# Wider mode products, one product for x, and shorter products on zeros in a windowed-attention and spectral-mixing kernel

## The chip, the cores and the metric

The kernel runs on one core of one Trainium2 chip. The metric is the device time of one execution in microseconds; the median of several executions counts. The engines are named as in the profile: PE is TensorE (PEld its weight loads), DVE is VectorE, ACT is ScalarE, POOL is GpSimd, and SP is SyncE, which only issues DMAs here.

## The reference

The kernel computes windowed causal attention and then mixes its output over the sequence in the frequency domain. Cut to what matters:

```python
# q, k, v: (8 batches, 8 heads, 576 positions, 64)
scores = where(0 <= i - j < 64, q @ k.T / 8, -1e9)
x = (softmax(scores) @ v), heads side by side    # (8, 576, 512)
X = rfft(x, axis=1)[:, :64]                       # 64 modes, Xr and Xi
Yr[m] = Xr[m] @ w_r[m] - Xi[m] @ w_i[m]           # w_r, w_i: (64, 512, 512)
Yi[m] = Xr[m] @ w_i[m] + Xi[m] @ w_r[m]
y = irfft(Y, n=576)
u = x + y
out = u + max(u @ w_ch, 0)                        # w_ch: (512, 512)
```

All inputs and the output are float32 in memory. The weights of the modes are 2 x 64 x 512 x 512 numbers, by far the most of what is read.

## The kernel before

The program is one stream per engine, in an order written out by hand; each engine runs its instructions in that order and waits on semaphores between engines.

**Products on zeros.** Right at the start (L428 to L432) a stretch of Yall is set to zero, and PE multiplies it with itself WARM = 8 times, 512 columns each, into a PSUM tile that nobody reads. Meanwhile SP fetches k and q of the first group as float32 (load_by_sp, L419), DVE computes the table of sines and then casts them (L426), and POOL issues the other loads.

**Attention (until about 196 us).** Sixteen groups (8 batches by two halves of the heads) pass through. transpose_raw (L292) turns k, q and v on PE in products of 64 columns (L298), and ACT copies them out (L302). The scores (L345), the subtraction of the maximum (L357), the turned weights (L365) and the product with v (L385) follow, and do_dft (L402) multiplies each finished half batch with the tables of cosines and sines, into XQ[0] and XQ[1], for the lower and upper 256 channels. All loads go through POOL's queue (load, L281, and load_weights, L150), cast to bfloat16 on the way. In POOL's order a load of k, q or v waits until PE has turned what lay in its buffer, and a load of weights until its buffer is spent.

**Modes.** A group is four modes. For every mode the weights are multiplied from the lower and upper channels (hb) and for the real and imaginary part (ri). Three forms of product exist. Each puts several products side by side on PE by tile_position, which gives each of them its own columns of the array:

- mode_half (L217), for the lower channels of groups 0 to 9 and the upper ones of groups 0 and 1: four modes side by side, 32 columns of weights each.
- mode_wide (L231), for the upper channels of groups 2 to 9 (WIDE = 2, EARLY = 10). The 256 rows of two modes lie interleaved, so that each load writes whole partitions; one tile of moving data holds both modes. The stationary side comes from XE, which holds one copy of X for the even and one for the odd mode (index h), with zeros in the rows of the other mode. For each of the NW = 4 slices j and each of the four modes g there is one product with 32 stationary columns: 16 products for each call, and 16 calls.
- mode_pair (L244), for the groups from 10 on.

The 32 columns are four slots of 8 batches. Slot by slot XE holds -Xi, Xr and Xi for each j, three slots each, and a product takes four slots in a row, from Xr on for ri = 0 and from -Xi on for ri = 1. The first two of the four are the answer, the last two are never read. wide_modes (L721) fills XE once, at about 202 to 207 us: products with a spreading matrix (L730), then a memset (L735), copies by ACT (L740) and negated copies by DVE (L741).

Between the mode products PE prepares the end: it turns tiles of x (L678), multiplies them with w_ch (L685), and DVE keeps the results as XW (L942). load_weights keeps POOL's queue filled; a load goes out when its ring buffer is free.

**Tail (from about 394 us).** After the last weights, 36 tiles of 128 positions are finished in pairs. For a pair PE brings XW into PSUM (L976), adds the inverse transform (L986, L993, L1033, L1063), and DVE, ACT and POOL add and store. rows_u (L1025) brings x itself into PSUM by a product with the identity, for the 12 tiles that are not in add_x: two products of 256 columns, one for each half of the channels (L1029), ahead of the inverse transform of the same tile (L1033). SP sends the finished tiles out (L1003).

Of the kernel before, what the change touches and what calls it, by code (L numbers as in the profile page):

```python
# [13 lines left out]
ALU = mybir.AluOpType  # L14
# [2 lines left out]

NRA = 3
NRB = 5
WARM = 8  # L20
NEG = -1.0e30
MAGIC = 12582912.0
PSAFE = 3.14159
# [3 lines left out]
def kernel(  # L27
# [10 lines left out]
    nc = tc.nc  # L38
    B, H, S, D = q.shape
# [9 lines left out]
    HALF = DM // 2  # L49
    NJ = 2  # L50
    NW = DM // 128
# [16 lines left out]
    ident_bf = consts.tile([128, 128], BF16, name="ident_bf")  # L68
# [19 lines left out]
    XQ[1] = post.tile([128, 3 * NJ + 2, B, NM], BF16, name="XQ1")  # L88
    XE = XQ[1].rearrange("p s b m -> p (s b m)")
    Yall = post.tile([2 * NM, B, DM], BF16, name="Yall")  # L90
# [14 lines left out]
    WIDE = 2  # L105
    NE = 2 * (EARLY - WIDE)
    SHARES = 25, 11, 80, 12
    assert sum(SHARES) == 128
    XE = XE[:, 0:2 * (3 * NW + 2) * B * NE].rearrange("p (h s b m) -> p h s b m", h=2, b=B, m=NE)
    ONES = 3, 0  # L110
    wlist = []
    for at, (grp, hb) in enumerate(steps):
        for ri in range(2):
            p = 4 * grp
# [26 lines left out]
    wtiles, spent = {}, set()  # L141
# [72 lines left out]
    def spend(at, ri):  # L214
        spent.update(i for i, w in enumerate(wlist) if w[0] == at and w[3] == ri)
# [15 lines left out]
    def mode_wide(psm, at, ri):  # L231
        grp, hb = steps[at]
        for j in range(NW):
            for g in range(4):
                nc.tensor.matmul(out=psm[32 * g:32 * g + 32, :],  # L235
                                 lhsT=XE[:, g % 2].rearrange("k s b m -> k (s b) m")[:, (3 * j + 1 - ri) * B:(3 * j + 5 - ri) * B,
                                                                                    2 * (grp - WIDE) + g // 2],
                                 rhs=wtiles[4 * grp + g - g % 2, hb, ri][:, j], start=(ri == 0 and j == 0),
                                 stop=(ri == 1 and j == NW - 1), tile_position=(0, 32 * g))
        for i in range(2):  # L240
            wtiles.pop((4 * grp + 2 * i, hb, ri))
        spend(at, ri)
# [19 lines left out]
    with tc.manual_schedule():  # L262
# [165 lines left out]
        idle = Yall[:, 0, :]  # L428
        nc.vector.memset(idle, 0.0)
        warm = ps_m.tile([128, DM], FP32, name="warm", tag="misc")  # L430
        for _ in range(WARM):
            nc.tensor.matmul(out=warm, lhsT=idle[:, 0:128], rhs=idle, start=True, stop=True)  # L432

        casts = list(load_by_sp(0, "k", Vflat[1])) + list(load_by_sp(0, "q", Vflat[2]))
        nc.gpsimd.iota(Kf, pattern=[[1, 64]], base=0, channel_multiplier=0,
# [11 lines left out]
        for nm in ("k", "q", "v"):  # L447
# [17 lines left out]
                         op0=ALU.max, op1=ALU.min)  # L465
# [82 lines left out]
        for it in range(-3, NU + 3):  # L548
# [23 lines left out]
            g = starts.get(it + 2)  # L572
# [3 lines left out]
            g = starts.get(it + 1)  # L576
# [34 lines left out]
        def bank(h, shape=(128, DM), dtype=FP32, name=None):  # L611
            return banks[h].tile(list(shape), dtype, name=name or "ps" + h, tag="bank")
# [50 lines left out]
        def group_y(b):  # L663
            return 32 * ((b // 2 + 2) % 4)
# [4 lines left out]
        def yrows(b):  # L669
            return Yall[:, b, :]  # L670
# [50 lines left out]
        def wide_modes():  # L721
            nc.vector.memset(sprE, 0.0)
            for r in range(2):
                for h in range(2):
                    nc.vector.tensor_copy(out=sprE[:, r, h, h::2], in_=ident_bf[:, r::2])
            pts = [[bank("zt"[r == 0]) for j in range(NJ)] for r in range(2)]
            for r in range(2):
                for j in range(NJ):
                    for h in range(2):
                        nc.tensor.matmul(  # L730
                            out=pts[r][j][:, 2 * B * NE * h:2 * B * NE * (h + 1)], lhsT=sprE[:, r, h],
                            rhs=XQ[1][:, 3 * j + 1:3 * j + 3, :, 4 * WIDE:4 * EARLY].rearrange(
                                "p t b (m h) -> p (t b) m h", h=2)[:, :, :, h],
                            start=(h == 0), stop=True, skip_group_check=True)
            nc.vector.memset(XE[:, :, 3 * NW:], 0.0)  # L735
            for r in range(2):
                for j in range(NJ):
                    i = 3 * (NJ * r + j)
                    px = pts[r][j].rearrange("p (h t b m) -> p h t b m", h=2, t=2, b=B)
                    nc.scalar.copy(out=XE[:, :, i + 1:i + 3], in_=px)  # L740
                    nc.vector.tensor_scalar(out=XE[:, :, i], in0=px[:, :, 1], scalar1=-1.0, scalar2=None, op0=ALU.mult)  # L741
            lo = 4 * (LAST - EARLY)
            nc.vector.tensor_copy(out=XL, in_=XA[:, :, :, lo:lo + 8])

# [180 lines left out]
        tiles = []  # L925
# [33 lines left out]
        ps, pu = {}, {}  # L959
# [65 lines left out]
        def rows_u(of):  # L1025
            for i in of:
                if i not in add_x:
                    for h in range(2):
                        nc.tensor.matmul(out=pu[i][:, HALF * h:HALF * h + HALF], lhsT=ident_bf, rhs=tiles[i][0][:, h],  # L1029
                                         start=(h == 0), stop=True, skip_group_check=True)  # L1030
                if len(tiles[i][1]) == 1:
                    (at, b), = tiles[i][1]
                    nc.tensor.matmul(out=pu[i], lhsT=trigI[:, at:at + 128], rhs=yrows(b), start=(i in add_x), stop=True,  # L1033
                                     skip_group_check=True)
            for i in of:
                if len(tiles[i][1]) == 2:
                    for h, (at, b) in enumerate(tiles[i][1]):
                        nc.tensor.matmul(out=pu[i][64 * h:64 * h + 64], lhsT=trigI[:, at + 64 * h:at + 64 * h + 64], rhs=yrows(b),
                                         start=(i in add_x), stop=True, skip_group_check=True, tile_position=(0, 64 * h))
            for i in of:  # L1040
                b = tiles[i][1][0][1]
                if len(tiles[i][1]) == 2 and b < NLB:
                    r = slice(group_y(b), group_y(b) + 32)
                    nc.tensor.matmul(out=pu[i], lhsT=trigX[r], rhs=YL[r], start=False, stop=True, skip_group_check=True,
                                     tile_position=(group_y(b), 0))
# [32 lines left out]
        def full_u(n):  # L1078
            banks_u(n)
            ut = uts[n] = new_ut()  # L1080
            joint = len(tiles[seq[n][0]][1]) == 2
            for of in [seq[n]] if joint else [(i,) for i in seq[n]]:
                rows_u(of)
                for i in of[0:1]:
                    take_rows(i, ut[:, seq[n].index(i)])
            tail_xw(n)
# [22 lines left out]
        def last(n):  # L1109
            banks_u(n)  # L1110
            ut = new_ut()
            ut = [ut[:, j] for j in range(2)]
            for j, i in enumerate(seq[n]):
                rows_u((i,))
                take_rows(i, ut[j])
            for j, i in enumerate(seq[n]):
                tail_xw(n, (j,))
                rows_z(i)
                for lo in range(0, DM, HALF * (2 - j)):
                    hi = lo + HALF * (2 - j)  # L1120
                    nc.vector.scalar_tensor_tensor(out=ut[j][:, lo:hi], in0=ps[i][:, lo:hi], scalar=0.0,
                                                   in1=ut[j][:, lo:hi], op0=ALU.max, op1=ALU.add)
                    done[i] = ut[j]
                    put_out(nc.scalar if lo else nc.sync, i, lo, hi)
# [8 lines left out]
        for i, (grp, hb) in enumerate(steps[EARLY:]):  # L1133
            if i == WIDE - 1:
                whole_modes()
            if i == WIDE:
                wide_modes()
# [13 lines left out]
            psm = bank("m")  # L1151
# [51 lines left out]
        for h, ps_ in enumerate(zl):  # L1203
            for c in range(NDCH):
                nc.tensor.matmul(out=ps_[:, 0:HALF], lhsT=trz[:, c].rearrange("p g k -> p (g k)"),
                                 rhs=wch[:, c, HALF * h:HALF * h + HALF], start=(c == 0), stop=(c == NDCH - 1))
# [8 lines left out]
        for g in (2, 3):  # L1215
            nc.sync.dma_start(out=Zall.bitcast(FP32)[rows, 2 * g:2 * g + 2],
                              in_=ZL.bitcast(FP32)[32 * g:32 * g + 32])
# [43 lines left out]
```

## Time and profile before

| | |
|---|---|
| median of 3 runs | 430.47 us (430.37 to 432.55) |
| profiled execution, its time | 430.37 us |
| its span, first to last instruction | 428.6 us |
| mean granted TensorE clock | 0.909 |
| PE busy, PE weight loads busy | 341.0 us (80%), 224.9 us (52%) |
| DVE, ACT, POOL busy | 247.1, 184.6, 113.2 us |
| DMA moved | 93.30 MB, 81.80 of them on POOL's queue |

A row of the timeline gives start, duration, engine, line, operation, the tile written and the tiles read, partitions and columns of the weights (128*32 is 128 rows and 32 columns), the shape written, and the count; in brackets stands how long the engine had been idle and for what. Where several instructions are merged into one row, the duration is that from the first start to the last end. A product's own duration includes the time that it takes to run through the array, so that products follow each other in less than one duration. A row of the chain of waits gives start, length and what the end was waiting for at that time. The windows view gives each engine's busy time in a stretch, the granted TensorE clock, and the DMA share, which is over 1 where packets overlap.

### The profile page before, as it was taken

Reading aid. Unit: us, or ns where it says so; the run is one execution under the profiler, and the core shown is the slowest. Engines: PE = TensorE matmul, PEld = TensorE weight load, DVE = VectorE, ACT = ScalarE, POOL = GpSimd, SP = SyncE. Lnnn points to the kernel's source line nnn. Section 1 sums busy time; section 2 is a strip of 40 time slices with the busy share of each in tenths; the row PEclk is TensorE's granted clock in tenths of the full one; section 3 lists DMA queues with packets and bytes.
Section 4 is the critical chain, followed back from the end, with each engine's and each line's share of the span. In section 5 each row is a group of like instructions: output and inputs, shape, how many; then the busy total and the mean of one; then the engine's idle time right before and its main releaser. Section 6 shows DMA issues by size and latency. Waiting matters only on the chain.

```text
span 428.6 us, 11742 instructions
## 1 busy us (share of the span) xinstructions
PE 341.0 (80%) x5098; PEld 224.9 (52%) x5142; DVE 247.1 (58%) x527; ACT 184.6 (43%) x334; POOL 113.2 (26%) x174
## 2 busy tenths in 40 slices
PE   6889989898999998987628577669675668878994
PEld 3656767676767676663204233346454445445552
DVE  8688777877677675784503212033322333886995
ACT  5655757575676566532401101025222214233663
POOL 8313223222122132112222222121111111120994
PEclk9999999999999999985657767689999986999998
DMA  8999999999999999999999999999999999996698
GB/s 206 211 211 212 211 212 210 212 211 212 211 211 212 213 213 210 213 213 214 213 255 220 213 213 214 207 211 214 214 215 214 214 214 214 213 210 119 241 364 299
DMA packets 37188, 93.30 MB, mean 218 GB/s; under 512 B 2992, under 2 KB 3248, under 8 KB 37136
## 3 DMA queue, kind: packets, MB, share of 16 engines
q0 software_dynamic: 31424, 81.80, 97.9%
q1 hardware_dynamic: 5568, 10.62, 6.8%
q8 instruction: 40, 0.66, 0.6%
q10 hardware_dynamic: 144, 0.13, 0.1%
q14 instruction: 12, 0.10, 0.1%
HBM read 163.58 MB, written 9.44 MB: 404 GB/s over the span
## 4 chain that ended last, share of the span: by engine, by line
DMA 43%; PE 39%; DVE 8%; issue 6%; ACT 3%; POOL 0%; DVEq 0%; SPq 0%; POOLq 0%; ACTq 0%
DMA wr<-in_moe_w_r_dram 23%; DMA wi<-in_moe_w_i_dram 16%; PE tr L298 6%; PE s L345 5%; DMA rawk<-in_k_dram 4%; PE s L357 4%; PE pt L365 4%; PE vb L310 3%; PE o L385 3%; PE s L337 2%; PE psm L223 2%; PE psz L685 2%; PE psm L254 2%; DVE xw L888 1%; PE px L408 1%
## 5 line engine op out<-in xcount | busy, mean ns | idle before, releaser
L685 PE MATMUL psz<-wch,tr 128*128 128x512 f32 x176 | 58.6, 462 | 10.8 <-DMA wch<-in_moe_w_ch_dram 10.0
L349 DVE TENSOR_REDUCE mx<-s 128x4 fp32r<-128x512 f32 x72 | 49.6, 688 | 25.5 <-PE s L345 25.2
L942 DVE CAST xw<-psz 128x512 fp32r<-128x512 f32 x36 | 24.9, 692 | 67.7 <-PE psz L685 67.7
L653 ACT CAST tr<-ptx 128x512 fp32r<-128x512 bf16 x36 | 21.2, 590 | 78.4 <-PE ptx L678 78.4
L359 ACT ACTIVATE p<-s 128x512 bf16<-128x512 f32 x72 | 39.7, 603 | 13.0 <-PE s L357 13.0
L685 PEld LDWEIGHTS psz<-wch,tr 128*128 128x128 f32 x176 | 34.4, 216 | 17.4 <-issue 10.2
L345 PE MATMUL s<-kT,qT 64*64 64x128 bf16 (+1 forms) x576 | 29.2, 221 | 6.7 <-issue 6.7
L302 ACT COPY kT<-tr 128x576 bf16<-128x576 bf16 x32 | 23.2, 724 | 21.4 <-PE tr L298 21.4
L368 DVE COPY pts<-pt 128x1024 bf16<-128x1024 bf16 (+1 forms) x40 | 25.2, 630 | 5.8 <-PE pt L365 4.3
L302 ACT COPY qT<-tr 128x576 bf16<-128x576 bf16 x32 | 23.3, 727 | 11.5 <-PE tr L298 11.5
L235 PEld LDWEIGHTS <-XQ 128*32 128x32 bf16 x256 | 11.4, 147 | 31.9 <-issue 25.5
L345 PEld LDWEIGHTS <-qT 64*64 64x64 bf16 x576 | 18.0, 107 | 17.7 <-issue 17.2
L357 PE MATMUL s<-mx,ident_r 128*128 128x512 f32 x72 | 26.2, 437 | 0.0
L302 ACT COPY vT<-tr 128x576 bf16<-128x576 bf16 x32 | 23.3, 728 | 4.7 <-PE tr L298 4.5
L285 POOL DMA_DIRECT2D rawk<-in_k_dram x15 | 8.1, 538 | 64.3 <-PE tr L298 56.3
L365 PE MATMUL pt<-ident_bf,p 128*128 128x128 bf16 x288 | 23.3, 220 | 1.8 <-issue 1.6
L747 DVE TENSOR_TENSOR stg<-psm,Yfour 128x512 bf16<-128x512 f32 x10 | 6.9, 689 | 30.6 <-PE psm L235 27.1
L254 PEld LDWEIGHTS <-XQ 128*32 128x32 bf16 x256 | 9.4, 149 | 28.4 <-issue 28.1
L235 PE MATMUL psm<-wi,XQ 128*32 128x512 bf16 x128 | 14.9, 507 | 10.5 <-DMA wi<-in_moe_w_i_dram 10.5
L184 POOL DMA_DIRECT2D wi<-in_moe_w_i_dram x14 | 9.5, 683 | 50.2 <-PE psm L254 29.1
L397 DVE TENSOR_TENSOR x_sb<-o,r 128x512 bf16<-128x512 f32 x32 | 22.1, 691 | 1.1
L235 PE MATMUL psm<-wr,XQ 128*32 128x512 bf16 x128 | 15.1, 540 | 7.4 <-DMA wr<-in_moe_w_r_dram 5.4
(277 smaller groups left out, 710.0 us busy)
## 6 DMA issues: line engine op xcount, KB each, us to landing
wi<-in_moe_w_i_dram POOLq DMA_DIRECT2D x21, 1024.0 KB, 14.3
wr<-in_moe_w_r_dram POOLq DMA_DIRECT2D x18, 1024.0 KB, 13.7
wi<-in_moe_w_i_dram POOLq DMA_DIRECT2D x17, 512.0 KB, 19.4
wr<-in_moe_w_r_dram POOLq DMA_DIRECT2D x16, 512.0 KB, 19.4
out_dram<-ut SPq DMA_DIRECT2D x29, 256.0 KB, 3.4
rawv<-in_v_dram POOLq DMA_DIRECT2D x16, 288.0 KB, 15.9
rawk<-in_k_dram POOLq DMA_DIRECT2D x15, 288.0 KB, 14.6
rawq<-in_q_dram POOLq DMA_DIRECT2D x15, 288.0 KB, 14.6
```

Source lines behind the costliest of these rows:

```text
L235: nc.tensor.matmul(out=psm[32 * g:32 * g + 32, :], lhsT=XE[:, g % 2].rearrange("k s b m -> k (s b) m")[:, (3 * j + 1 - ri) * B:(3 * j + 5 ...
L298: nc.tensor.transpose(out=pt[ro, j, :], in_=raw[ro, TH * half + j, :], identity=ident_bf[ro, ro])
L302: nc.scalar.copy(out=to, in_=pt.rearrange("p j n -> p n j"))
L345: nc.tensor.matmul(out=s[ro, t, lo:128], lhsT=lq, rhs=kT[ro, 64 * n - 64 + lo:64 * n + 64], start=False, stop=True, skip_group_check=True)
L349: nc.vector.tensor_reduce(out=mx, in_=s, axis=AX.X, op=ALU.max, negate=True)
L357: nc.tensor.matmul(out=s, lhsT=ident_r, rhs=mx.unsqueeze(2).to_broadcast([128, 4, 128]), start=False, stop=True, skip_group_check=True)
L359: nc.scalar.activation(out=p[:, 4 * c2:4 * c2 + 4, :], in_=s, func=ACT_F.Exp, scale=EX_SCALE)
L365: nc.tensor.transpose(out=pt[:, t, :], in_=st[u]["p"][:, t, :], identity=ident_bf)
L368: nc.vector.tensor_copy(out=ps[:, 0:nt, :], in_=pt[:, 0:nt, :])
L397: nc.vector.tensor_tensor(out=xo.rearrange("p c (h d) -> p c h d", d=64), in0=ov[:, :, :, 0:64], in1=rb, op=ALU.mult)
L685: nc.tensor.matmul(out=pz, lhsT=tr[:, c, :], rhs=wch[:, c, :], start=(c == 0), stop=(c == NDCH - 1))
L942: nc.vector.tensor_copy(out=XW[i], in_=multiply(tr))
```

## The change

Three edits. The number of products on zeros goes from 8 to 58, and each has 64 columns, not 512; each has a weight load of its own, as before. In mode_wide one product takes both modes of an interleaved pair: 64 stationary columns, eight slots in a row, two products side by side instead of four, 8 for each call instead of 16. For this XE loses its index h and has seven slots for each j: -Xi, Xr, Xi of the even mode, a slot of zeros, and -Xi, Xr, Xi of the odd one. The four last slots of a product still hold what is never read, or the zeros. The zeros take a second memset. In rows_u the two products for x of a tile become one of 512 columns. In the order of instructions PE has 180 rows fewer (products and weight loads), DVE has one more, and POOL, ACT and SP have the same.

```diff
--- before.py
+++ after.py
@@ -17,7 +17,7 @@
 
 NRA = 3
 NRB = 5
-WARM = 8
+WARM = 58
 NEG = -1.0e30
 MAGIC = 12582912.0
 PSAFE = 3.14159
@@ -106,7 +106,7 @@
     NE = 2 * (EARLY - WIDE)
     SHARES = 25, 11, 80, 12
     assert sum(SHARES) == 128
-    XE = XE[:, 0:2 * (3 * NW + 2) * B * NE].rearrange("p (h s b m) -> p h s b m", h=2, b=B, m=NE)
+    XE = XE[:, 0:(7 * NW + 2) * B * NE].rearrange("p (s b m) -> p s b m", b=B, m=NE)
     ONES = 3, 0
     wlist = []
     for at, (grp, hb) in enumerate(steps):
@@ -231,12 +231,12 @@
     def mode_wide(psm, at, ri):
         grp, hb = steps[at]
         for j in range(NW):
-            for g in range(4):
-                nc.tensor.matmul(out=psm[32 * g:32 * g + 32, :],
-                                 lhsT=XE[:, g % 2].rearrange("k s b m -> k (s b) m")[:, (3 * j + 1 - ri) * B:(3 * j + 5 - ri) * B,
-                                                                                    2 * (grp - WIDE) + g // 2],
-                                 rhs=wtiles[4 * grp + g - g % 2, hb, ri][:, j], start=(ri == 0 and j == 0),
-                                 stop=(ri == 1 and j == NW - 1), tile_position=(0, 32 * g))
+            for i in range(2):
+                nc.tensor.matmul(out=psm[64 * i:64 * i + 64, :],
+                                 lhsT=XE.rearrange("k s b m -> k (s b) m")[:, (7 * j + 1 - ri) * B:(7 * j + 9 - ri) * B,
+                                                                           2 * (grp - WIDE) + i],
+                                 rhs=wtiles[4 * grp + 2 * i, hb, ri][:, j], start=(ri == 0 and j == 0),
+                                 stop=(ri == 1 and j == NW - 1), tile_position=(0, 64 * i))
         for i in range(2):
             wtiles.pop((4 * grp + 2 * i, hb, ri))
         spend(at, ri)
@@ -429,7 +429,7 @@
         nc.vector.memset(idle, 0.0)
         warm = ps_m.tile([128, DM], FP32, name="warm", tag="misc")
         for _ in range(WARM):
-            nc.tensor.matmul(out=warm, lhsT=idle[:, 0:128], rhs=idle, start=True, stop=True)
+            nc.tensor.matmul(out=warm[:, 0:64], lhsT=idle[:, 0:128], rhs=idle[:, 0:64], start=True, stop=True)
 
         casts = list(load_by_sp(0, "k", Vflat[1])) + list(load_by_sp(0, "q", Vflat[2]))
         nc.gpsimd.iota(Kf, pattern=[[1, 64]], base=0, channel_multiplier=0,
@@ -732,13 +732,15 @@
                             rhs=XQ[1][:, 3 * j + 1:3 * j + 3, :, 4 * WIDE:4 * EARLY].rearrange(
                                 "p t b (m h) -> p (t b) m h", h=2)[:, :, :, h],
                             start=(h == 0), stop=True, skip_group_check=True)
-            nc.vector.memset(XE[:, :, 3 * NW:], 0.0)
+            nc.vector.memset(XE[:, 0:7 * NW].rearrange("p (j s) b m -> p j s b m", s=7)[:, :, 3], 0.0)
+            nc.vector.memset(XE[:, 7 * NW:], 0.0)
             for r in range(2):
                 for j in range(NJ):
-                    i = 3 * (NJ * r + j)
+                    i = 7 * (NJ * r + j)
                     px = pts[r][j].rearrange("p (h t b m) -> p h t b m", h=2, t=2, b=B)
-                    nc.scalar.copy(out=XE[:, :, i + 1:i + 3], in_=px)
-                    nc.vector.tensor_scalar(out=XE[:, :, i], in0=px[:, :, 1], scalar1=-1.0, scalar2=None, op0=ALU.mult)
+                    xe = [XE[:, i + t:i + t + 8].rearrange("p (h s) b m -> p h s b m", h=2) for t in range(2)]
+                    nc.scalar.copy(out=xe[1][:, :, 0:2], in_=px)
+                    nc.vector.tensor_scalar(out=xe[0][:, :, 0], in0=px[:, :, 1], scalar1=-1.0, scalar2=None, op0=ALU.mult)
             lo = 4 * (LAST - EARLY)
             nc.vector.tensor_copy(out=XL, in_=XA[:, :, :, lo:lo + 8])
 
@@ -1025,9 +1027,8 @@
         def rows_u(of):
             for i in of:
                 if i not in add_x:
-                    for h in range(2):
-                        nc.tensor.matmul(out=pu[i][:, HALF * h:HALF * h + HALF], lhsT=ident_bf, rhs=tiles[i][0][:, h],
-                                         start=(h == 0), stop=True, skip_group_check=True)
+                    nc.tensor.matmul(out=pu[i].rearrange("p (h e) -> p h e", h=2), lhsT=ident_bf, rhs=tiles[i][0],
+                                     start=True, stop=True, skip_group_check=True)
                 if len(tiles[i][1]) == 1:
                     (at, b), = tiles[i][1]
                     nc.tensor.matmul(out=pu[i], lhsT=trigI[:, at:at + 128], rhs=yrows(b), start=(i in add_x), stop=True,
```

## Prediction

> **What bounds the kernel now.** I read the page first: the span, then the DMA row and the queues, and only after that the engines.
>
> ```profile
> span 428.6 us, 11742 instructions
> ...
> DMA  8999999999999999999999999999999999996698
> GB/s 206 211 211 212 211 212 210 212 211 212 211 211 212 213 213 210 213 213 214 213 255 220 213 213 214 207 211 214 214 215 214 214 214 214 213 210 119 241 364 299
> ...
> q0 software_dynamic: 31424, 81.80, 97.9%
> ```
>
> Each digit is 10.7 us. From the second slice to the 36th the DMA engines are full, at 206 to 220 GB/s almost throughout (255 in the one slice that holds the uncast load of w_ch). One queue, POOL's, carries 81.8 of the 93.3 MB. So the time has two parts: a stream of loads that ends when the last weights land, and a tail that computes and writes the result. The chain of waits shows the joint:
>
> ```profile
> 393.78 0.44 PE psm L254 x4
> 394.22 0.67 PE pst L976 x2
> ```
>
> The last mode products (L254) start when their weights land, at 393.78. The tail is 428.6 - 393.8 = 34.8 us. PE bounds it up to 413; from 404 on the result is written at 380 GB/s, and the chain ends in the writes. An edit moves the end only if it leaves the load queue empty, or shortens or lengthens the tail. To drain the queue is not easy: loads take a median of 14 to 19 us from issue to landing, while at 0.21 MB per us a load of 1 MB needs 5.
>
> **Part 1, the products on zeros (L432).** Before, 8 products of 512 columns; after, 58 of 64, each with its own weight load. The head of the timeline:
>
> ```profile
> 1.19 3.60 PE L432 MATMUL warm<-Yall 128*128 128x512 bf16 x8 [1.19 <-DVE Yall L429]
> ...
> 5.44 0.69 PE L298 MATMUL tr<-ident_bf,rawk 64*64 64x64 bf16 x18 [0.65 <-DVE rawk L426]
> ...
> 7.61 0.69 PE L298 MATMUL tr<-ident_bf,rawq 64*64 64x64 bf16 x18 [1.48 <-DVE rawq L426]
> ...
> 9.08 0.56 POOL L285 DMA_DIRECT2D rawk<-in_k_dram  x1 [0.26 <-PE tr L298]
> ```
>
> The long ones start 0.427 us apart (512 columns at half clock; in the tail 512 take 0.22), and end at 4.79. PE then waits 0.65 us for DVE's cast of k. The nearest row to a short one is L755: also 128x128 weights, also 64 columns, in fours.
>
> ```profile
> 207.66 0.40 PE L755 MATMUL psp<-sel,stg 128*128 128x64 bf16 x4
> ```
>
> One of them takes up to 0.242 us in its source row, so the four start (0.40 - 0.242)/3 = 0.053 us apart (64 columns at half clock). 58 x 0.053 = 3.1 us: the block ends near 1.19 + 3.1 + 0.2 = 4.5 us, before the cast. Cost: 0. Bounds for one product: below, 0.036 us (L755's four weight loads take 0.24 us with 0.132 for one), 2.1 us in all; above, a weight load of 0.152 (L432's source row) and 0.053 one after the other, 0.205, 11.9 us in all, ending at 13.1. I take 0.053, the row of that very shape.
>
> If the clock rises earlier than now (transposes go 18 in 0.69 us up to 12 us, and 18 in 0.45 from 13.15, so now it rises near 12.9), PE gains at most half of its 5.3 busy us between 5.4 and 13: 2.6 us. What hides gain or loss is the queue. At 9.08 POOL issues the first load that waits for PE. By then 3.4 MB are issued (four of 0.29, one of 1.05, two of 0.59 from SP) and 1.87 have moved by the windows' rates, so 1.5 MB or 7.3 us are still queued, up to 16.4 us. A block that ends by about 14 us leaves no hole. POOL's own instructions and their waits are the same in both kernels.
>
> **Part 2, the modes of groups 2 to 9 (L235).** 16 calls of mode_wide, each now 8 products of 64 columns of weights in place of 16 of 32; 128 products and 128 weight loads fewer. Per call PE makes four rounds over 512 columns either way: four products side by side before, two after. The rows of old and of nearest new form:
>
> ```profile
> 228.96 1.93 PE L235 MATMUL psm<-wr,XQ 128*32 128x512 bf16 x16
> ...
> 232.51 1.09 PE L235 MATMUL psm<-wi,XQ 128*32 128x512 bf16 x16
> ```
>
> ```profile
> 414.34 0.41 PE L1038 MATMUL psy<-Yall,trigI 128*64 128x512 bf16 x2
> 414.58 0.38 PE L1038 MATMUL psp<-Yall,trigI 128*64 128x512 bf16 x2
> ```
>
> One old product lasts 0.38 at full clock, so 16 in 1.09 are (1.09 - 0.38)/3 = 0.24 a round. In L1038 two 64-column tiles run fully side by side (two products of 0.38 in 0.38 to 0.41), and the next two start 0.24 later: the same round. So I take no change of PE time. Bounds: below, two rounds of four saved, -0.48 us a call; above, no pairing, +4 x 0.22 = 0.9 at full and 4 x 0.43 = 1.7 at half clock, 14 to 27 us over 16 calls. Cover: from 210 to 280 us PE is busy 43.6 of 70 us, while DMA's share stays at 1.05 or more. The gain is lost in waiting for weights (19.2 us of DMA in the chain at 210, 229 and 249); a loss fits into 26 idle us, but for the upper end.
>
> The set-up (L735 to L741) has one memset more, and its first is as large as before (256 words, 0.27 us at 204.11), the second half of it, some 0.2 us by the same row. DVE waits 0.31 us for ACT right behind them now, at 204.69: hidden, and if not, 0.2 us on a stage with a full queue.
>
> **Part 3, x by one product (L1029).** This is the only edit in the tail. 12 tiles, each with 2 products of 256 columns now and 1 of 512 after.
>
> ```profile
> 400.93 0.39 PE L1029 MATMUL psm<-x_sb,ident_bf 128*128 128x256 bf16 x2
> ...
> 401.16 0.38 PE L1033 MATMUL psm<-Yall,trigI 128*128 128x512 bf16 x1
> 401.37 0.38 PE L1029 MATMUL psm<-x_sb,ident_bf 128*128 128x256 bf16 x2
> ```
>
> The pair holds PE from 400.93 to 401.16, 0.23 us; the 512-column product behind it from 401.16 to 401.37, 0.21. The weight loads lie beside products. Gain 0.02 x 12 = 0.24 us of PE time; but PE bounds only the 8 tiles up to 413, and the writes already run near their rate then. I take 0.1. Bounds: 0, and 12 x 0.11 = 1.3 if one of the two vanished entirely.
>
> **Sum.** 0 + 0 - 0.1, against the profiled execution: 430.37 us, of which 428.6 are span and 1.8 lie around it. 430.37 - 0.1 = 430.3. The median of the three runs shown is 430.47, 0.1 higher; one of them took 432.55. The bound of 0.5% used below is 2.15 us, about what a measurement of this kernel can tell from no change.
>
> **Rivals.**
> - *PE, not the queue, paces the first 196 us* (faster). PE is busy 0.9 and more there, and POOL waits 56 us for L298 ahead of k's loads. Then an earlier clock counts in full: 2.6 + 0.1, 427.7 us. Against it: the DMA share is 1.11 in every window from 9 us on, and PE itself waits for a load of k (1.3 us at 167). 0.09.
> - *The block on zeros becomes late work* (slower): one weight load after another at the head of PE. At 0.205 a product the first transposes start at 13.1, 5.5 us after both casts are ready. If the queue runs dry for it, up to 430.4 + 5.5 = 435.9. It decides only from about 14 us on, as worked out above, or if PE paces the stage. For it: no row shows 58 such loads behind one another. Against: L755. 0.07. The Trainium skill ("TensorE: Matmul & The Clock Gate", LDWEIGHTS) gives a weight load as its columns over 1.2, which would be an estimated 107 ns here and 6.2 us for the block, to 7.4. The fours of L755 at 36 ns a load speak against it, and by it the rawq transposes would slip some 0.5 us, 430.9 at most.
> - *The 64-column products do not pair.* PE needs 14 to 27 us more against 26 idle; the excess and a late start of the work from 282 on might cost 3 us, 433. Against: L1038. 0.04.
> - *The new form gains on PE but nothing follows*: that is the forecast, 430.3, and it has 0.72.
> - *Scatter as in the run of 432.55*, with a time between 431 and 432.6: 0.08, half of it over the bound.
>
> Faster by over 0.5%: 0.09, the first rival. Slower: 0.07 less 0.03 for a small slip, 0.04 and 0.04, together 0.12. Same: 0.79. The range takes in 1.3 us for part 3 below (429.0), and the scatter above (432.6).
>
> **What would show it.** After: L432's 58 products end by 5 us and the first L298 still starts at 5.4; a call of L235 still takes 1.0 to 1.1 us at full and 1.9 at half clock, with half the count; the last L254 starts at 393.8 within 0.5; a 512-column L1029 holds PE 0.21 us; the tail is 34.7. Wrong would be: a DMA digit below 9 ahead of slice 36, an L432 block past 7.6 us, or last weights landing before 392.

## The result and the profile after

The changed kernel takes 431.99 us in the median of 20 runs (431.47 to 433.38), the kernel before 430.40 (430.05 to 432.55). The ratio is 1.0033, with a 95% interval of 1.0025 to 1.0042: slower by 1.6 us, clear of the scatter, though inside the half per cent. The time lies in the range that was given, but on the other side of the forecast of 430.3.

The lines of the page after that answer to those shown of before:

```profile
span 430.6 us, 11564 instructions
...
DMA  8999999999999999999999999999999999994887
GB/s 203 211 212 211 212 211 211 211 212 213 210 212 212 211 212 212 213 213 214 214 259 214 213 214 214 207 214 215 214 214 214 216 213 215 210 214 84 301 324 269
...
q0 software_dynamic: 31424, 81.80, 97.3%
```

The load queue is as full as it was. Up to slice 36 the two DMA rows agree digit by digit, and GB/s within a few; only the last four slices differ, where the tail lies. In the timeline of after the last weights land at the same time:

```profile
393.86 0.44 PE L254 MATMUL psm<-wi,XL 128*32 128x256 bf16 x4 [0.81 <-DMA wi<-in_moe_w_i_dram]
```

That is 0.08 us later than before. So the tail went from 428.6 - 393.8 = 34.8 to 430.6 - 393.9 = 36.7 us, and all but a trifle of the 2.0 us by which the spans differ arose in it. (The profiled execution of after took 432.33 us, a little over its median.)

**What is new in the tail** is found by asking the waits view for PE alone, from 394 us on. Before it has one line, after two (engine and line, whom it waited for, us in total, times, longest):

```profile
PE psm L254 <- DMA wi<-in_moe_w_i_dram: 0.5, 1, 0.5
```

```profile
PE psm L1030 <- DVE x_sb L1009: 1.9, 2, 1.5
PE psm L254 <- DMA wi<-in_moe_w_i_dram: 0.8, 1, 0.8
```

L1030 is the product for x (L1029 before). It now waits twice for DVE's sums at L1009 (L1007 before). Around the two places the timeline of after reads:

```profile
400.09 1.28 DVE L1009 TENSOR_TENSOR x_sb<-psm,x_sb 128x512 f32<-128x512 f32 x2
...
401.42 0.38 PE L1030 MATMUL psm<-x_sb,ident_bf 128*128 128x512 bf16 x1 [0.36 <-DVE x_sb L1009]
...
404.21 0.39 PE L1030 MATMUL psm<-x_sb,ident_bf 128*128 128x512 bf16 x1
...
404.46 0.68 DVE L1009 TENSOR_TENSOR x_sb<-psy,x_sb 128x512 f32<-128x512 f32 x1
```

```profile
407.02 0.39 PE L1030 MATMUL psm<-x_sb,ident_bf 128*128 128x512 bf16 x1
...
410.07 0.68 DVE L1009 TENSOR_TENSOR x_sb<-psy,x_sb 128x512 f32<-128x512 f32 x1
...
410.67 0.68 DVE L1009 TENSOR_TENSOR x_sb<-psp,x_sb 128x512 f32<-128x512 f32 x1
...
411.41 0.39 PE L1030 MATMUL psm<-x_sb,ident_bf 128*128 128x512 bf16 x1 [1.52 <-DVE x_sb L1009]
```

The products follow the sums' ends (401.37 and 411.35) by some 0.05 us. In between, at 404.21, one starts ahead of a sum into the same tile x_sb and is not held. The same steps before:

```profile
406.76 0.39 PE L1029 MATMUL psm<-x_sb,ident_bf 128*128 128x256 bf16 x2
...
409.57 0.39 PE L1029 MATMUL psm<-x_sb,ident_bf 128*128 128x256 bf16 x2
```

Before, 2.81 us lie between the x products of the 9th and the 11th pair; after, 411.41 - 407.02 = 4.39. That is 1.58 us lost at one place. At the first place 401.42 - 400.93 = 0.49 had been lost, the later landing included. Of this, 0.23 were regained by 404, since the kernel before stood still there anyway, until DVE had read out a PSUM bank that PE's next product was to fill:

```profile
402.14 0.19 PEld L976 LDWEIGHTS pst<-xw,ident_r 128*128 128x128 f32 x1 [0.35 <-DVE ut L1014]
```

So 0.26 remained. From the 11th pair to the last issue of a write nothing changes any more; here it is before and after, 1.82 us apart:

```profile
424.21 0.37 ACTq L1003 DMA_DIRECT2D out_dram<-ut  x1
```

```profile
426.03 0.39 ACTq L1005 DMA_DIRECT2D out_dram<-ut  x1
```

From there to the end of the span it takes some 0.2 us longer (4.39 and 4.57).

**Why the product waits.** x_sb lies in memory as [half of the channels][batch][4 chunks][256], 8192 numbers to a half. The x of a tile of batch 4 to 7 lies in both halves; its operand for one product reaches from an address of 4096 or more in the lower half to 12288 or more in the upper one. Between these lie, in the upper half from 8192 to 12287, the places of batches 0 to 3, and these are where the sums of the early tiles with c = 2 are kept (UE, L912 after). The product reads none of them, which two separate products show by needing no wait. The places of c = 0, in the lower half below 4096, lie outside. Theory A: the wait comes where a write falls between the first and the last address of an operand, even if the operand skips that place. The rivals: B, the wider mode products or the products on zeros cost the time; C, the longer product does; D, the wait goes with the pairs (a PSUM bank, DVE's order) and not with the address.

### The profile page after: what moved, and what is told of

Read it like the earlier page. It is cut to its first block, busy times and chain, and to the rows that moved or that the text cites. A ratio compares the mean times of both kernels' runs of the same rounds, so it can differ in the third digit from the quotient of the medians.

```text
span 430.6 us, 11564 instructions
## 1 busy us (share of the span) xinstructions
PE 337.1 (78%) x5008; PEld 228.0 (53%) x5052; DVE 246.4 (57%) x528; ACT 184.8 (43%) x334; POOL 113.7 (26%) x174
## 5 line engine op out<-in xcount | busy, mean ns | idle before, releaser
L235 PEld LDWEIGHTS <-XQ 128*64 128x64 bf16 x128 | 14.8, 203 | 29.6 <-issue 23.8
L254 PEld LDWEIGHTS <-XQ 128*32 128x32 bf16 x256 | 9.4, 149 | 28.1 <-issue 27.9
L235 PE MATMUL psm<-wi,XQ 128*64 128x512 bf16 x64 | 14.4, 511 | 12.1 <-DMA wi<-in_moe_w_i_dram 12.1
L298 PE MATMUL tr<-ident_bf,rawk 64*64 64x64 bf16 x576 | 15.1, 196 | 7.0 <-DMA rawk<-in_k_dram 4.9
```

The costliest lines, as they stand in the source:

```text
L235: nc.tensor.matmul(out=psm[64 * i:64 * i + 64, :], lhsT=XE.rearrange("k s b m -> k (s b) m")[:, (7 * j + 1 - ri) * B:(7 * j + 9 - ri) * B, ...
```

## The experiments

Line numbers in the diffs' kernels shift by a few. Each set of kernels was timed beside the kernel before on the same chip: it took 430.71 us beside e1 to e4 and beside e5 to e8, and 430.67 beside e9. The ratios are those on record with their 95% intervals; they are not the quotients of the two medians.

**e1 and e2: the parts apart.** e1 is the changed kernel with the old rows_u, e2 the old kernel with the new one.

```diff
-                    nc.tensor.matmul(out=pu[i].rearrange("p (h e) -> p h e", h=2), lhsT=ident_bf, rhs=tiles[i][0],
-                                     start=True, stop=True, skip_group_check=True)
+                    for h in range(2):
+                        nc.tensor.matmul(out=pu[i][:, HALF * h:HALF * h + HALF], lhsT=ident_bf, rhs=tiles[i][0][:, h],
+                                         start=(h == 0), stop=True, skip_group_check=True)
```

> The changed kernel with x of a tile by two products of 256 columns again; the products on zeros and the 64-column mode products stay changed. Theory A: all the loss comes from PE's wait in the tail (0.36 us at 401.4 and 1.52 us at 411.4, for DVE's sums into x_sb), which the one product for x brings in, because its operand spans from the lower-channel half of x_sb to the upper one, and between the two lie the upper-channel places of batches 0 to 3, into which DVE is writing the sums of the tiles with c = 2. Then: as the kernel before, 430.4 within 0.4 us, no PE wait for x_sb in the tail. Rival B: the loss comes from the wider mode products or the products on zeros, and the waits in the tail only take up slack: 431.5 or more, last weights landing later than 394. Rival C: the longer product as such delays DVE and ACT: also 430.4 here, so this run doesn't tell C from A.

> The kernel before with only x by one product of 512 columns. Theory A: 432.0 within 0.5 us, PE waiting for DVE's sum into x_sb ahead of the x product of the 5th and of the 11th pair, about 0.4 and 1.5 us, nothing else moved. Rival B: 430.4. Rival C: 432.0 too, but without such waits.

e1 took 430.65 us, ratio 0.9995 (0.9984 to 1.0007), and PE has no wait for x_sb in its tail. e2 took 432.58, ratio 1.0050 (1.0033 to 1.0067), just above the 432.5 at which its forecast ended. Its x products:

```profile
401.44 0.38 PE L1028 MATMUL psm<-x_sb,ident_bf 128*128 128x512 bf16 x1 [0.35 <-DVE x_sb L1007]
...
411.42 0.39 PE L1028 MATMUL psm<-x_sb,ident_bf 128*128 128x512 bf16 x1 [1.52 <-DVE x_sb L1007]
```

The same two waits, to 0.01 us, without the other two edits. B is out: part 3 alone brings the loss, and parts 1 and 2 together bring none that shows.

**e3 and e4: the pairs in another order.** The one product stays in e3. The sums into the upper half come two places ahead of the 5th pair's x products before, three in e3; the later ones, directly ahead of the 11th pair before, come behind it in e3. e4 is the yardstick, the old kernel in the same order.

```diff
-        AA = [(tile_of(b, c), tile_of(b + 2, c)) for b in range(NLB // 2) for c in range(4)]
+        AA = [(tile_of(b, c), tile_of(b + 2, c)) for b in range(NLB // 2) for c in ((0, 2, 1, 3), (0, 1, 3, 2))[b]]
```

> The changed kernel with the early pairs of the tail in another order: c = 0, 2, 1, 3 for batches 0 and 2, and 0, 1, 3, 2 for 1 and 3, so that no pair with an x product follows a c = 2 pair directly. The one product for x stays. Theory A: no PE wait for x_sb in the tail, 430.3 within 0.6 us (and within 0.5 of the next kernel, the same order with the product in two). Rival C: the loss stays with the longer product, 432. Rival B: 432.

> The kernel before with the same new order of the early pairs, as the yardstick for the run before: what the order alone does. All theories: within 0.5 us of 430.4, since PE bounds the tail up to 413 and its work is the same; the order of what is written out shifts a little.

e3: 430.97 us, ratio 1.0002 (0.9991 to 1.0013); e4: 430.78, 1.0003 (0.9991 to 1.0014). In e3 PE's only wait in the tail is the one for weights:

```profile
PE psm L254 <- DMA wi<-in_moe_w_i_dram: 0.8, 1, 0.8
```

The loss is gone with the long product still there, so C is out. It also gains nothing over e4. (The time is 0.07 above the 430.9 at which the forecast for e3 ended, but that forecast went by 430.4 for the kernel before; to e4 it is 0.19.)

**e7: only the places exchanged.** Here D is put to the test. Work and order are those of the changed kernel; one index decides in which half of x_sb a sum lies.

```diff
-                        UE[i] = x_sb[:, c // 2, b].rearrange("p c e -> p (c e)").bitcast(FP32)
+                        UE[i] = x_sb[:, 1 - c // 2, b].rearrange("p c e -> p (c e)").bitcast(FP32)
```

> The changed kernel with one index changed: the sums of the early tiles with c = 0 lie in the upper-channel half of x_sb and those with c = 2 in the lower one, the other way round than now. No work and no order changes, only where DVE writes. Theory A, the address between the two halves decides: the waits ahead of the x products of the 5th and 11th pair vanish, and one of 1.0 to 1.7 us comes ahead of the 7th pair, which follows the c = 0 pair of batches 1 and 3, near 404 us; 431.5 to 432.2. Rival D, PE waits there for something that goes with the pairs and not with the place (a PSUM bank, the order of DVE): waits of 0.4 and 1.5 us stay at the 5th and 11th pair, 432.2.

432.06 us, ratio 1.0029 (1.0014 to 1.0044). The x products of the 5th, 7th, 9th and 11th pair in its timeline, with the sums ahead of the first two:

```profile
400.57 1.28 DVE L1009 TENSOR_TENSOR x_sb<-psm,x_sb 128x512 f32<-128x512 f32 x2
...
401.48 0.39 PE L1030 MATMUL psm<-x_sb,ident_bf 128*128 128x512 bf16 x1
...
405.54 0.68 DVE L1009 TENSOR_TENSOR x_sb<-psp,x_sb 128x512 f32<-128x512 f32 x1
...
406.27 0.39 PE L1030 MATMUL psm<-x_sb,ident_bf 128*128 128x512 bf16 x1 [1.71 <-DVE x_sb L1009]
...
409.08 0.39 PE L1030 MATMUL psm<-x_sb,ident_bf 128*128 128x512 bf16 x1
...
411.89 0.39 PE L1030 MATMUL psm<-x_sb,ident_bf 128*128 128x512 bf16 x1
```

Both old waits are gone. The product at 401.48 starts while the sums of c = 2, now in the lower half, run on to 401.85. A wait of 1.71 us stands ahead of the 7th pair, which was never held before and which now follows the sums into the upper half; its product starts 0.05 us behind their end (406.22). The wait goes with the address. D is out. The runs don't show what sets the wait, nor whether the region that it guards ends exactly at the operand's first and last address. It isn't the whole upper half: of two separate products the second reads there too, and is not held.

**e8: two products in two pairs.**

```diff
+                    if i in (*seq[4], *seq[10]):
+                        for h in range(2):
+                            nc.tensor.matmul(out=pu[i][:, HALF * h:HALF * h + HALF], lhsT=ident_bf, rhs=tiles[i][0][:, h],
+                                             start=(h == 0), stop=True, skip_group_check=True)
+                    else:
+                        nc.tensor.matmul(out=pu[i].rearrange("p (h e) -> p h e", h=2), lhsT=ident_bf, rhs=tiles[i][0],
+                                         start=True, stop=True, skip_group_check=True)
```

> The changed kernel with x by two products in the 5th and the 11th pair of the tail only, by one product in the other eight tiles. Theory A: no PE wait for x_sb, 430.5 within 0.5 us, the same as with two products everywhere. Rival C (the longer product costs by itself): two thirds of the loss stay, 431.5.

430.53 us, ratio 0.9988 (0.9975 to 1.0000), no wait for x_sb. Four of the twelve tiles carry the whole loss.

**e5 and e6: parts 1 and 2 alone,** in the old kernel.

> The kernel before with only the products on zeros changed: 58 of 64 columns. Theory A (the loss is all in part 3) and the forecast's part 1: 430.5 within 0.5 us, the block ends before 4.8 us. Rival: the block costs or gains something of its own that part 2 hides in e1, then over 0.5 us away.

> The kernel before with only the 64-column mode products. Theory A and the forecast's part 2: 430.5 within 0.5 us; a call of 8 products takes 1.0 to 1.1 us at full and 1.9 to 2.1 at half clock. Rival: over 0.5 us away, with part 1 making up for it in e1.

e5: 431.46 us, ratio 1.0011 (0.9999 to 1.0022). The median lies 0.75 us above the kernel before and 0.96 above the 430.5 expected, outside the half microsecond allowed, but the interval of the ratio touches 1; a loss of up to 0.2% by the products on zeros is neither shown nor excluded. e6: 430.55, ratio 0.9985 (0.9974 to 0.9997), a gain of 0.15% with an interval that ends just below 1. e1, with both, is at 0.9995. The two rows that part 1 and part 2 forecast, first e5's block on zeros and its first transposes, then two calls of mode_wide in the timeline of the changed kernel:

```profile
1.19 3.27 PE L432 MATMUL warm<-Yall 128*128 128x64 bf16 x58 [1.19 <-DVE Yall L429]
5.34 0.47 PE L298 MATMUL tr<-ident_bf,rawk 64*64 64x64 bf16 x18 [0.87 <-DVE rawk L426]
```

```profile
228.81 1.98 PE L235 MATMUL psm<-wr,XQ 128*64 128x512 bf16 x8
...
233.14 1.03 PE L235 MATMUL psm<-wr,XQ 128*64 128x512 bf16 x8
```

**e9: the best of the parts.** The 64-column mode products, x as in e8, and the old eight long products on zeros.

> What the runs so far leave as the best choice: the 64-column mode products, x by one product except in the 5th and the 11th pair, and the old 8 long products on zeros. If the small gains of those two parts (0.1% each, at the edge of their intervals) are real and add up, 429.8 to 430.2 beside 430.6 for the kernel before; if they are scatter, 430.6 within 0.3.

430.24 us against 430.67, ratio 0.9987 (0.9978 to 0.9996). That lies between the two forecasts, and a tenth of a per cent below the kernel before, hardly clear of the scatter. Since e6 has as much without any change to x, the mode products are the likely source, but this isn't shown: e1 has them too, and no gain that shows. Why fewer instructions there should save time was not tried.

## Why the prediction was wrong

**The step that failed is part 3.** "0.02 x 12 = 0.24 us of PE time ... I take 0.1", with bounds of 0 and 1.3, priced the product and nothing else. It never asked what else the new operand touches, and so excluded a loss without a reason. In its place the runs show waits of PE, 0.36 and 1.52 us long, for writes that lie between the two halves of the operand (e2 has them alone, e7 moves them with the address, e3 and e8 remove them). What was to be looked at stands in the kernel: x_sb is one tile, its lower and upper half were two operands, and DVE writes sums into the same tile one or two pairs earlier. That the time lies in the range all the same is luck: the upper end of the range was there for scatter. The prediction's own check, that POOL's instructions and waits are the same in both kernels, was made on the wrong engine.

**The small gain of part 3 isn't there either.** After, the long product at 404.21 and the one behind it at 404.44 are 0.23 apart, as the pair and the product behind it were. The iterations without a wait last 2.81 us in both kernels.

**What held.** The queue: full to slice 36 in both, last weights at 393.78 and 393.86. That the tail is where an edit counts, and that PE bounds it up to 413: a stop of 1.52 us came through as 1.58. Part 1: the block ends at 1.19 + 3.28 = 4.47 in the profile of after, where 4.5 was forecast. One of its products takes 0.242 in its source row, so the 58 go (3.28 - 0.242) / 57 = 0.053 us apart, as forecast from the row of the same shape. The Trainium skill's rule of columns over 1.2 for a weight load ("TensorE: Matmul & The Clock Gate", LDWEIGHTS), an estimated 107 ns for these, is twice too much as the pace of a load and its product. As the time of a single load it agrees: the block's source row has 106 to 132 ns. Part 2: 1.03 at full clock and 1.98 at half, where 1.0 to 1.1 and 1.9 stood.

One sign came out otherwise. The first transposes were to start at 5.4 as before; in the profile of after they started at 6.59:

```profile
6.59 0.69 PE L298 MATMUL tr<-ident_bf,rawk 64*64 64x64 bf16 x18 [2.12 <-DVE rawk L426]
```

They waited for DVE's cast, not for the block, which had ended at 4.47. Both starts occur with either block: 5.34 in e5 with the new one, 6.57 in e9 with the old. By the third row of transposes nothing is left of it (8.09 after, 8.11 before).

**The rivals.** PE as what paces the first 196 us: the profiles speak against it. The first mode products behind the last transform of the attention start 1.09 us earlier after than before:

```profile
194.56 1.11 PE L223 MATMUL psm<-wr,XQ 128*32 128x512 bf16 x8 [0.64 <-ACT XQ L414]
```

```profile
193.47 1.10 PE L223 MATMUL psm<-wr,XQ 128*32 128x512 bf16 x8 [0.64 <-ACT XQ L414]
```

The last weights landed 0.08 us later all the same. In e9 these products start at 193.31, 1.25 us earlier than before, and the weights landed at 393.61, 0.17 earlier. An early clock is no matter of the block either: the first 18 transposes took 0.47 us in e5, with the new block, and in e2, with the old one. The block on zeros as late work, and 64-column products that don't pair, are refuted by the rows of the block and of mode_wide. None of the rivals had the wait. The chances stood at 0.79 for a change within half a per cent, which is what came, and 0.12 for a greater loss; the mechanism of the loss had none.

## What to carry to other kernels

Before two accesses are merged into one with a stride, look at what lies between their pieces and who writes there at that time: a wait may come in for data that the access never touches. If it does, two remedies removed it here at no cost that could be seen: another order of the steps (e3) and two accesses at just the spots that are hit (e8). Exchanging the places of the writes only moved the wait (e7). And when an edit takes instructions from the engine that bounds a stage, compare that engine's waits before and after first; here 0.02 us a product was to be saved, and the new wait was 1.5.

## What the runs showed of the hardware

A weight load of 64 columns out of XE takes 0.194 to 0.223 us in the changed kernel, and one of 32 columns took 0.135 to 0.170 in the kernel before (source rows of L235). A load of 128 columns of ident_bf, which lie side by side, takes 0.095 to 0.100 (L1029). XE's columns lie 16 numbers apart and fill only a part of the array; which of the two makes the loads longer was not tried. The longer loads don't show in the time of a call, since they overlap each other and the products. At full clock the sixteen of two calls take 1.61 us, where one after the other they would take at least 16 x 0.194 = 3.1:

```profile
232.16 1.61 PEld L235 LDWEIGHTS <-XQ 128*64 128x64 bf16 x16 [0.37 <-issue]
```
